# Second-stage 49x49 blocks on quarters of the TensorE array

## The chip, the cores and the metric

The kernel runs on one core of a Trainium2 chip. A core has five engines that work side by side, each through its own list of instructions in order: TensorE (PE: matmuls, 128 rows by 128 columns of multipliers), ScalarE (ACT), VectorE (DVE), GpSimd (POOL) and SyncE (SP, which here only issues DMAs). A matmul takes a stationary operand of up to 128 rows and 128 columns, streams up to 512 columns of a moving operand through it, and writes to PSUM, an accumulator memory of eight banks, each 128 partitions by 512 float32. ACT and DVE copy results from PSUM to SBUF. The metric is device time in microseconds.

## The reference

Two blocks follow each other, for eight batches of 3136 rows by 256 columns. The first is an attention whose weights are the squared positive part of the scores; the second projects its result three ways, convolves one projection with a long filter (by FFT over the 3136 rows), gates it twice and projects again.

```python
scores = (1.0 / S) * np.matmul(z, z.transpose(0, 2, 1))      # S = 3136, z has 64 columns
attn = np.maximum(scores, 0.0) ** 2
x = u * np.matmul(attn, v)
proj = x @ w_proj                                            # 256 -> 768
x1, x2, x3 = proj[..., :D], proj[..., D:2 * D], proj[..., 2 * D:]
x2_conv = np.fft.irfft(np.fft.rfft(x2, n=S, axis=1) * np.fft.rfft(filter_fft, n=S, axis=0)[None], n=S, axis=1)
out = (x1 * x2_conv * x3) @ w_out
```

## The kernel before

**Attention.** The columns of a batch's scores are cut into seven chunks (CHUNKS: five of 512, then 256 and 320), the rows into 25 tiles of 128. A *unit* of scores is two tiles (four in the chunk of 256) against one chunk. `score_mm` computes it with matmuls of 64 contraction rows: z is held twice, on partitions 0 to 63 and 64 to 127, so that one block uses the upper rows of the array and the next the lower rows, and each block goes to a bank of its own. A unit's two banks are one of three *pairs* (`ps_s`). ACT then takes the ReLU of both banks at once (tile R_t, line 1681), ACT or DVE squares it (A_t, lines 1688 and 1690), and `weigh` multiplies the squares with v into `ps_o`, two banks that collect a chunk. Scores are symmetric: some squares are turned by DMA transposes on SP's queue (M_t, M2e_t, M2o_t, line 1616) and used again in a later chunk. A short last tile of 64 rows goes through `weigh_short`.

**Projection and convolution.** A finished chunk becomes xT_t (line 1732), is projected with `wp` and gated (line 1062), and the part to convolve goes through a DFT in two stages, since 3136 is 64 x 49. Stage one (`dft1`, matrix T) is a full-array matmul; its result s_t goes to a scratch in DRAM (`spec`). When the seven chunks of a batch are through, `add_spectrum` reads the scratch back in another order (`load_spec`, tile spec_in_t). Stage two has 32 blocks of 49 x 49 per batch, each with 256 columns of real and imaginary parts side by side. `forward` multiplies the blocks of S, DVE multiplies with the filter's spectrum H (line 1161) and combines (1165, 1166), `inverse` multiplies the transposed blocks TZ, and the result gs_t goes to the scratch again (line 1212). In the last batch the combination is left out and `inverse2` does it by twice as many matmuls, with a negated copy of TZ (`make_minus`). `add_end` reads the second scratch, applies T4, gates (line 1255), multiplies with `wo` and stores.

**The second stage before.** Two blocks make one *slot* j of 16 (NJ). Their rows lie interleaved on 98 partitions (KR), and a stationary operand of 98 x 100 (KC) holds both blocks, with zeros where a row and a column belong to different blocks (`masks`). So a slot is one full-array matmul of 512 columns into one bank; slot 0, with the two frequencies that are their own mirror images, needs four matmuls of 256 columns and three more matrices (`sums`). `forward`, `inverse` and `inverse2` are called by tasks of kind FB that take one bank (`one_slots`); ACT or DVE copies it out (`both`).

**What sets the order.** No scheduler of the compiler is used. The class `Plan` holds estimated costs of all tasks and simulates the engines while it emits the instructions. `pick_pe` chooses what TensorE does next from queues of kinds: S (scores), W (weighted sums), FA, FB and FZ (projection, spectrum, ends). It starts a run of scores when two or three pairs of banks are free and stays in it while the next pair is. `go` adds 0.095 us where scores and other work follow each other. `Pairs` and `Singles` keep account of the banks of `ps_s`: a task takes a whole pair or one bank (MOST bounds the single ones). `pick` decides between ACT and DVE for jobs that both can do (YIELD weighs how long a job that only the other engine can do is held up).

**Lines of the profile.** All matmuls are issued by one helper and stand under line 468, transposes under 471; copies by ACT stand under 501 and by DVE under 505. In names, S and TZ are the matrices of stage two, zT_t the scores' operand, v_t the weighted sums' stationary operand.

Of the kernel before, what the change touches and what calls it, by code (L numbers as in the profile page):

```python
# [21 lines left out]
KR = 2 * N2  # L22
KC = 100
# [6 lines left out]
BACKLOG, AMPLE, STAY = 1.5, 5.0, 0.05  # L30
LATE_PUT, LATE_LOAD, LATE_TURN, LATE_C, LATE_D2 = 3.0, 1.0, 1.5, 2.5, 1.0
SPEC_LAG = 1
LATE_F = 6.0
AFTER = (1, 3, 5, 6)
FINAL = (0, 2, 4, 6, 1, 3, 5)
ZP, ZL = 0, 0.0
MOST = 3
FULL = INF
YIELD = 0.0
# [46 lines left out]
class Banks:  # L86
# [5 lines left out]
    def settle(self, k, t):  # L92
        self.at[k[0]][k[1]] = t

# [67 lines left out]
class Plan:  # L162


    def __init__(self):
        self.free = {e: 0.0 for e in ("PE", "ACT", "DVE", "SP", "POOL")}
        self.queues = {"S": [], "W": [], "FA": [], "FB": [], "FZ": []}
        self.pend = {e: [] for e in ("ACT", "DVE", "SP", "POOL")}
        self.credit = 0.0
        self.mode = None  # L170
        self.n = 0
        self.spare = []
        self.pairs = None
        self.bus = 0.0
# [74 lines left out]
    def pick_pe(self):  # L249
        t = self.free["PE"]  # L250
        got = {}
        for k, window in (("S", 1), ("W", 1), ("FA", 6), ("FB", 6), ("FZ", 6)):
            best = None
            for task in self.queues[k][:window]:
                s = max(t, self.ready_at(task))
                if s < INF and (best is None or s < best[0] - 1e-9):
                    best = (s, task)
            if best:
                got[k] = best
        if not got:  # L260
            return None
        more = self.queues["S"]
        if more and not more[0].left:
            left = self.backlog()
            if self.mode == "S":
                if "S" in got and got["S"][0] <= t + STAY:
                    return (*got["S"], "S")
                got.pop("S", None)
            else:
                want = 3 if left > AMPLE else 2  # L270
                free = self.pairs.when(min(want, len(more)) - 1)
                if "S" in got and free > t + 0.04:
                    rest = {k: v for k, v in got.items() if k != "S" and (k == "W" or left > BACKLOG)}
                    if rest and min(v[0] for v in rest.values()) < free:
                        got = rest
                    elif free < INF:
                        return max(got["S"][0], free), got["S"][1], "S"
            if not got:
                return None
        near = t + 0.04  # L280
        order = ["S"]
# [29 lines left out]
    def go(self):  # L311
        while True:
# [11 lines left out]
            if k:  # L324
                self.queues[k].remove(task)
                if (k == "S") != (self.mode == "S") and self.mode:
                    start += 0.095
                self.mode = k
# [10 lines left out]
def kernel(  # L339
# [133 lines left out]
    pair_slots, one_slots = Pairs(banks), Singles(banks)  # L473
# [132 lines left out]
    nc.gpsimd.iota(k1v, pattern=[[N2, N1 // 2], [0, 2]], base=0, channel_multiplier=0)  # L606
# [111 lines left out]
    pf, tp, odd, ge, php, n1p, pa, pb, r0, r1, m0, m1, half = (col[:, ds(i, 1)] for i in range(13))  # L718
    T1 = const.tile([P, P], BF16, name="T1")
    T4 = const.tile([P, P + N1], BF16, name="T4")  # L720
    NS = NJ + 3
    S2 = const.tile([P, NS, KC], BF16, name="S2")
    TZ = const.tile([P, NS, KC], BF16, name="TZ")
# [17 lines left out]
    def percol2():  # L741
        nc.vector.tensor_scalar(r1, pf, 0.5, -0.25, ALU.mult, ALU.add)
        nc.vector.tensor_scalar(r1, r1, RND, RND, ALU.add, ALU.subtract)
        nc.vector.tensor_scalar(tp, pf, 0.25, -0.375, ALU.mult, ALU.add)
        nc.vector.tensor_scalar(tp, tp, RND, RND, ALU.add, ALU.subtract)
        nc.vector.scalar_tensor_tensor(odd, tp, -2.0, r1, ALU.mult, ALU.add)
        nc.vector.scalar_tensor_tensor(r1, r1, -2.0, pf, ALU.mult, ALU.add)
        nc.vector.tensor_scalar(r0, r1, -1.0, 1.0, ALU.mult, ALU.add)
        nc.vector.tensor_scalar(tp, tp, -1.0, float(NT - 1), ALU.mult, ALU.add)
        nc.vector.tensor_tensor(m1, odd, r0, ALU.mult)  # L750
        nc.vector.tensor_tensor(m0, r0, m1, ALU.subtract)
        nc.vector.tensor_tensor(php, tp, r1, ALU.mult)
        nc.vector.tensor_scalar(php, php, float(NJ), float(QUART), ALU.mult, ALU.add)
        nc.vector.scalar_tensor_tensor(php, odd, -float(QUART), php, ALU.mult, ALU.add)
        nc.vector.tensor_single_scalar(half, pf, 0.0, ALU.is_equal)
        nc.vector.tensor_single_scalar(ge, pf, 25.0, ALU.is_equal)
        nc.vector.tensor_tensor(half, half, ge, ALU.add)
# [56 lines left out]
    s2_zero = on("POOL", lambda: nc.gpsimd.memset(S2[:].rearrange("p s m -> p (s m)").bitcast(F32), 0.0), 2.0, lat=0.3)  # L814
    after(s2_zero, 13.0)
    s2_done = []
    for j0 in (0, 8):
        box = {}

        def first(m, j0=j0):  # L820
            if j0:
                nc.vector.scalar_tensor_tensor(php, tp, 8.0, php, ALU.mult, ALU.add)
            nc.vector.tensor_scalar(m[:, 0 : 8 * N2], k2v, tp, php, ALU.mult, ALU.add)

        def masks(j0=j0, box=box):
            v = box["v"][:KR, 0 : 8 * N2].rearrange("p (j k) -> p j k", k=N2)
            a = int(j0 == 0)
            nc.vector.tensor_scalar(S2[:KR, ds(3 + j0 + a, 8 - a), 0:N2], v[:, a:], r0[:KR], None, ALU.mult)
            nc.vector.tensor_scalar(S2[:KR, ds(3 + j0, 8), 50 : 50 + N2], v, r1[:KR], None, ALU.mult)

        _, ta = sin_steps(box, 8 * N2, first, at=S2_AT)
        t = step("DVE", masks, 0.8)
        t.frees.append((ta, 0))
        if j0 == 0:
            join(t, s2_zero)
        s2_done.append(t)

    def q0_first(m):
        nc.vector.scalar_tensor_tensor(php, tp, -8.0, php, ALU.mult, ALU.add)
# [4 lines left out]
    def q0_masks():  # L844
        for i, msk, lo in ((3, m0, 0), (0, m0, 25), (1, m1, 0), (2, m1, 25)):
            nc.vector.tensor_scalar(S2[:KR, i, ds(lo, 25)], q0["v"][:KR, ds(lo, 25)], msk[:KR], None, ALU.mult)
        nc.vector.tensor_copy(S2[:KR, 2, 50:KC], S2[:KR, 3, 50:KC])

# [5 lines left out]
    for i0 in range(0, NS, 8):  # L854
        n = min(8, NS - i0)
        box = {}

        def turn(i0=i0, n=n, box=box):
            box["p"] = bank(BF16)
            for i in range(n):  # L860
                transpose(box["p"][:KC, ds(i * KR, KR)], S2[:KR, i0 + i, :], ident[:KR, :KR])

        def back(e, i0=i0, n=n, box=box):
            src = box["p"][:KC, 0 : n * KR].rearrange("p (s k) -> p s k", k=KR)
            copy(e, TZ[:KC, ds(i0, n), 0:KR], src)

        tt = pe("FB", turn, c_pe(*[P] * n), [s2_done[-1]], takes=[one_slots])
        tb = job(None, back, {"DVE": c_dve2(n * KR)}, [tt], prio=3)
# [3 lines left out]
    def halve():  # L872
        nc.vector.tensor_scalar(TZ[:KC, 0:4, 0:KR], TZ[:KC, 0:4, 0:KR], half[:KC], None, ALU.mult)

    tz_done.append(on("DVE", halve, 0.4, tz_done[:1], prio=3))
# [3 lines left out]
    def make_minus():  # L879
        minus.append(zT_p.tile())  # L880
        t = minus[0][:KC, 0 : NS * KC].rearrange("p (s k) -> p s k", k=KC)
        minus.append(t)
        nc.vector.tensor_single_scalar(t[:, :, 0:KR], TZ[:KC, :, 0:KR], -1.0, ALU.mult)

# [38 lines left out]
    def by_row(d):  # L923
        return d[0:S, :].rearrange("(p x) d -> p x d", x=2 * NJ)

    def load_spec(src, j0, nj, deps, late=0.0, home=l_p):
        box = {}

        def go():
            box["t"] = home.tile([P, 8, D] if home is l_p else [P, 4, D], BF16)  # L930
            nc.sync.dma_start(out=box["t"][:KR, 0 : 2 * nj, :], in_=by_row(src)[:, ds(2 * j0, 2 * nj), :])

        t = on("SP", go, 0.45, [*deps, *((d, ISSUED) for d in loads[-1:])], [home.slots], moves=0.6 * nj, late=late)
# [15 lines left out]
    def sums(ps, terms):  # L949
        for c, some in enumerate(terms):  # L950
            for k, (w, x) in enumerate(some):
                matmul(ps[:, ds(c * D, D)], w, x, start=(k == 0), stop=(k == len(some) - 1))

# [3 lines left out]
    def forward(ps, x, j):  # L957
        w = [S2[:KR, i, :] for i in range(NS)]
        if j:
            matmul(ps[:KC, :], w[3 + j], x, start=True, stop=True)  # L960
            return
        a, b = sides(x)
        sums(ps[:KC], (((w[3], a), (w[0], b)), ((w[1], a), (w[2], b))))

    def inverse(ps, y, j):
        w = [TZ[:KC, i, 0:KR] for i in range(NS)]
        if j:
            matmul(ps[:KR, :], w[3 + j], y, start=True, stop=True)
            return
        a, b = sides(y)  # L970
        sums(ps[:KR], (((w[3], a), (w[1], b)), ((w[0], a), (w[2], b))))

    def inverse2(ps, y, z, j):
        w = [TZ[:KC, i, 0:KR] for i in range(NS)]
        m = [minus[1][:, i, 0:KR] for i in range(NS)]
        (a, b), (c, d) = sides(y), sides(z)
        if j:
            sums(ps[:KR], (((w[3 + j], a), (m[3 + j], d)), ((w[3 + j], b), (w[3 + j], c))))
            return
        sums(  # L980
            ps[:KR],
            (
                ((w[3], a), (m[3], d), (w[1], b), (w[1], c)),
                ((w[0], a), (m[0], d), (w[2], b), (w[2], c)),
            ),
        )

    def c_line(j):
        return c_pe(2 * D) if j else c_pe(D, D, D, D)
# [12 lines left out]
    for j0 in range(0, NJ, 4):  # L1002
        ld, ibox = load_spec(DF, j0, 4, puts, LATE_F)
        for i in range(4):
            box = {}

            def mm(i=i, j0=j0, box=box, ibox=ibox):
                box["p"] = bank()
                x = ibox["t"][:KR, ds(2 * i, 2), :].rearrange("p c d -> p (c d)")
# [816 lines left out]
```

## Time and profile before

| | |
|---|---|
| median of 3 runs | 1012.26 us (1011.74 to 1012.39) |
| the profiled execution | 1012.86 us |
| its span, first to last instruction | 1011.0 us |
| granted clock of TensorE over the span | 0.997 of full speed |
| matmuls recorded | 5,958 (weight loads: 6,046) |
| matmuls of scores, 64 rows, 512 columns | 776 |
| second stage, 512 columns, forward (spec_in_t, S) | 122 |
| second stage, 512 columns, inverse (xh, TZ) | 105 |
| ReLU of 1024 columns on ACT | 408 x 1.031 us |
| squares of 1024 columns: on ACT, on DVE | 195 x 1.070 us, 197 x 1.221 us |
| HBM read and written | 142 GB/s over the span |

A group of the profile reads: line, engine, operation, output tile and input tiles, shape, count, busy time, mean of one. A matmul's shape stands as rows*columns of the stationary operand, then partitions x columns of the moving one. Some records of matmuls are missing (compare the count of weight loads), and a matmul's recorded duration includes a modelled end, so that matmuls that follow each other overlap in the table: what one costs is the distance from start to start. In the timeline, a row merges instructions of one group that follow each other: start, length, engine, group, count.

### The profile page before, as it was taken

What the parts mean: (1) busy time and instruction counts of PE and PEld (TensorE: products, weight loads), DVE (VectorE), ACT (ScalarE), POOL (GpSimd) and SP (SyncE); (2) the same over time, 40 slices, a digit from 0 to 9 for tenths busy, and PEclk for the clock granted to TensorE, in tenths of its full rate; (3) what the DMA queues carried; (4) which work ended last, traced back from release to release, by engine and by line L of the source; (5) the groups of instructions that cost most, each with busy time, mean ns of one, the idle gap of its engine ahead of it and who ended that gap; (6) DMA issues with size and microseconds to landing.
All of it is one profiled execution on the core that took longest, in us unless ns stands there. A gap on an engine that the chain in (4) does not pass through costs nothing.

```text
span 1011.0 us, 17656 instructions
## 1 busy us (share of the span) xinstructions
PE 967.4 (96%) x5958; PEld 490.8 (49%) x6046; DVE 787.6 (78%) x1424; ACT 907.9 (90%) x1231; POOL 188.7 (19%) x401
## 2 busy tenths in 40 slices
PE   6999999998999999999999999999999999999985
PEld 2344544455444564445544464445644455444654
DVE  7976779866797777887788777897769877797675
ACT  6988899998999899998999989998899989999774
POOL 5142311131011310123112131112201222000000
PEclk9999999999999999999999999999999999999998
DMA  9799868878978887987989889897888779977656
GB/s 167 141 175 171 160 132 163 161 155 172 181 165 168 167 182 163 175 136 150 213 180 161 154 180 211 144 187 168 194 166 169 153 133 207 201 142 162 132 187 207
DMA packets 331770, 170.18 MB, mean 168 GB/s; under 512 B 241160, under 2 KB 306504, under 8 KB 331680
## 3 DMA queue, kind: packets, MB, share of 16 engines
q1 hardware_dynamic: 303952, 138.09, 62.3%
q0 software_dynamic: 27728, 30.97, 21.1%
q8 instruction: 47, 0.77, 0.3%
q14 instruction: 43, 0.35, 0.1%
HBM read 90.26 MB, written 53.35 MB: 142 GB/s over the span
## 4 chain that ended last, share of the span: by engine, by line
PE 76%; DVE 8%; ACT 8%; issue 3%; DMA 3%; SPq 1%; ACTq 0%; DVEq 0%
PE ps_o_t L468 42%; PE ps_s L468 33%; ACT R_t L1681 5%; DVE A_t L1690 3%; ACT A_t L1688 2%; DVE xh L1161 1%; DVE xT_t L1732 1%; DMA out_dram<-ost_t 1%; DMA ost_t<-in_z_dram 1%; DMA M_t<-A_t 1%; DMA A_t<-spec 1%; SPq L593 1%; DVE yT_t L1255 0%; DVE R_t L1161 0%; ACT s_t L501 0%
## 5 line engine op out<-in xcount | busy, mean ns | idle before, releaser
L1681 ACT ACTIVATE R_t<-ps_s 128x1024 f32<-128x1024 f32 (+4 forms) x512 | 471.0, 958 | 43.9 <-PE ps_s L468 40.3
L468 PE MATMUL ps_o_t<-A_t,v_t 128*128 128x512 bf16 (+3 forms) x1998 | 461.7, 353 | 8.9 <-DVE A_t L1690 4.0
L468 PEld LDWEIGHTS <-v_t 128*128 128x128 bf16 x2826 | 254.3, 98 | 254.3 <-issue 59.4
L1690 DVE TENSOR_TENSOR A_t<-R_t 128x1024 bf16<-128x1024 f32 (+3 forms) x250 | 280.0, 1130 | 123.3 <-ACT R_t L1681 122.0
L1688 ACT ACTIVATE A_t<-R_t 128x1024 bf16<-128x1024 f32 (+3 forms) x246 | 243.2, 995 | 4.6 <-DMA M_t<-A_t 1.3
L468 PE MATMUL ps_s<-zT_t 64*128 64x512 bf16 (+2 forms) x1064 | 148.7, 356 | 4.8 <-ACT ost_t L501 2.7
L551 POOL COPY tick<-xT_t 1x1 bf16<-1x1 bf16 x54 | 14.0, 259 | 727.1 <-DVE xT_t L1732 727.1
L468 PE MATMUL ps_s<-xT_t,wp 128*128 128x512 bf16 (+2 forms) x418 | 102.3, 352 | 3.9 <-DVE xT_t L1732 1.9
L1732 DVE SCALAR_TENSOR_TENSOR xT_t<-ps_o_t,uT_t 128x256 bf16<-128x256 f32 (+2 forms) x224 | 76.1, 382 | 19.3 <-PE ps_o_t L468 18.5
L501 ACT ACTIVATE x_t<-ps_s 128x512 bf16<-128x512 f32 (+2 forms) x143 | 77.2, 572 | 15.4 <-PE ps_s L468 9.3
L468 PEld LDWEIGHTS <-zT_t 64*128 64x128 bf16 (+1 forms) x1081 | 43.4, 94 | 96.0 <-issue 81.0
L1161 DVE TENSOR_TENSOR xh<-xh,H 100x1024 bf16<-100x1024 bf16 x120 | 80.9, 683 | 3.7 <-ACT xh L501 3.3
L1062 DVE TENSOR_TENSOR gate_t<-ps_s,x_t 128x256 bf16<-128x256 f32 (+2 forms) x214 | 70.2, 382 | 16.9 <-PE ps_s L468 12.1
L468 PE MATMUL ps_o_t<-M_t,v_t 128*128 128x512 bf16 (+2 forms) x352 | 82.0, 353 | 0.1
L468 PEld LDWEIGHTS <-wp 128*128 128x128 bf16 x448 | 42.2, 97 | 48.5 <-issue 11.9
L1255 DVE TENSOR_TENSOR yT_t<-ps_s,gate_t 128x512 bf16<-128x512 f32 (+2 forms) x99 | 59.3, 619 | 3.5 <-PE ps_s L468 2.8
L542 POOL DMA_DIRECT2D un_t<-in_u_dram x112 | 60.0, 556 | 8.3 <-issue 6.1
L561 POOL DMA_DIRECT2D v_t<-in_v_dram x112 | 59.5, 553 | 4.1 <-issue 1.8
L468 PE MATMUL ps_s<-wp,xT_t 128*128 128x256 bf16 x398 | 56.4, 273 | 0.1
L468 PE MATMUL ps_s<-wo,yT_t 128*128 128x256 bf16 (+1 forms) x358 | 53.5, 273 | 1.4 <-DVE yT_t L1255 0.9
L501 ACT ACTIVATE xh<-ps_s 100x512 bf16<-100x512 f32 (+1 forms) x85 | 50.3, 632 | 2.3 <-PE ps_s L468 2.2
L505 DVE CAST x_t<-ps_s 128x512 bf16<-128x512 f32 (+2 forms) x70 | 44.6, 648 | 9.0 <-PE ps_s L468 7.1
(154 smaller groups left out, 884.6 us busy)
## 6 DMA issues: line engine op xcount, KB each, us to landing
out_dram<-ost_t SPq DMA_DIRECT2D x66, 256.0 KB
spec<-s_t SPq DMA_DIRECT2D x96, 128.0 KB
spec_in_t<-spec SPq DMA_DIRECT2D x28, 392.0 KB
spec<-gs_t SPq DMA_DIRECT2D x28, 392.0 KB
v_t<-in_v_dram POOLq DMA_DIRECT2D x80, 128.0 KB, 4.3
un_t<-in_u_dram POOLq DMA_DIRECT2D x80, 128.0 KB, 4.6
conv_in_t<-spec SPq DMA_DIRECT2D x33, 256.0 KB
out_dram<-ost_t SPq DMA_DIRECT2D x19, 128.0 KB
```

Of the source, the lines that this page charges most:

```text
L468: wrote(nc.tensor.matmul(o, *args, **kw), o)
L501: got = nc.scalar.activation(out_, in_, AF.Copy)
L505: got = nc.vector.tensor_copy(out_, in_)
L542: nc.gpsimd.dma_start(out=t[ds(j * N1, N1), lo - t0 : hi - t0, :], in_=x[:, n2 : n2 + hi - lo, :])
L561: nc.gpsimd.dma_start(out=t[ds(j * N1, N1), ds(v_at(a), (b - a) * D)], in_=r[:, n2 + a - lo : n2 + b - lo, :].rearrange("p t d -> p (t d)"),)
L1062: got = nc.vector.tensor_tensor(g[:, ::-1] if h == 0 else g, p, x, ALU.mult)
L1161: nc.vector.tensor_tensor(x[:, 1 - i], x[:, 0], h, ALU.mult)
L1255: got = nc.vector.tensor_tensor(yb["y"][:, dh, 0:w], p, gates[b, c, dh][:, 0:w], ALU.mult)
L1681: has_read(nc.scalar.activation(blocks(box["R"], n, cw)[:rows], p, AF.Relu), p)
L1688: nc.scalar.activation(a, r, AF.Square)
L1690: nc.vector.tensor_tensor(a, r, r, ALU.mult)
L1732: nc.vector.scalar_tensor_tensor(x, f, inv_s2, ut, ALU.mult, ALU.mult)
```

## The change

The second stage is laid out anew. The 49 rows of one block lie on partitions 0 to 48, those of the next on 64 to 112. A *unit* of four blocks is two slots: the block in row half h and slot c uses the 64 x 64 part of the array at rows h*64 and columns c*64, streams 512 columns and writes to partitions c*64 and up of bank h of a pair. The masks are gone, S2 holds the blocks as such, and three small matrices S0 and T0Z serve the two special frequencies. Where a unit has more than one matmul per part, the four parts take turns.

```diff
+    def quads(ps, plan_of):
+        todo = [(h, c, plan_of(h, c)) for h in range(2) for c in range(2)]
+        for n in range(max(len(x) for _, _, x in todo)):
+            for h, c, x in todo:
+                if n < len(x):
+                    cols, w, m, start, stop = x[n]
+                    matmul(ps[ds(c * N1, N1), h, cols], w, m, start=start, stop=stop)
...
-    def forward(ps, x, j):
-        w = [S2[:KR, i, :] for i in range(NS)]
-        if j:
-            matmul(ps[:KC, :], w[3 + j], x, start=True, stop=True)
-            return
-        a, b = sides(x)
-        sums(ps[:KC], (((w[3], a), (w[0], b)), ((w[1], a), (w[2], b))))
+    def forward(ps, x, i):
+        def of(h, c):
+            at = ds(h * N1, N2)
+            w, m = S2[at, 2 * i + c, :], x(c)[at]
+            if i or h or c:
+                return whole(w, m)
+            a, b = sides(m)
+            v = [S0[at, k, :] for k in range(3)]
+            return sums((((w, a), (v[0], b)), ((v[1], a), (v[2], b))))
+
+        quads(ps, of)
```

`inverse` and `inverse2` change likewise. A unit is a task of a new kind Q, which takes a pair of banks and is copied out by two jobs, one for each bank (`Half` and `Halves` free each bank by itself). The same function serves the filter, the forward and the inverse pass:

```diff
+    def add_quads(mm, ev, cost, deps, takes):
+        box = {}
+
+        def go():
+            box["p"] = ps_t[plan.got[0][1]]
+            mm(box["p"])
+
+        a = pe("Q", go, cost, deps, [pair_slots, *takes])
+        evs = []
+        for h in range(2):
+            e_ = job(None, lambda e, h=h: ev(e, h, box["p"][:, h, :]), both(2 * D), [a])
+            e_.frees.append((Half(a, half_slots, h), 0))
+            evs.append(e_)
+        return a, evs
```

Units are put into runs of scores. When a run begins and a unit is due (`soon`), the whole run goes on quarters: each score matmul of 128 stationary columns is issued as two of 64 columns, and so is the short last tile.

```diff
+            o = blocks(ps, len(pair), cw)[:, i]
+            for m in range(0, P, N1 if plan.quarters else P):
+                n = N1 if plan.quarters else P
+                matmul(o[ds(m, n)], zt[h, ds(t * P + m, n)], zt[h, ds(C0[at], cw)], start=True, stop=True)
```

In `pick_pe`, while a run on quarters lasts, one unit follows the first score unit (LEAD = 1, `quad_run`), and more only when no scores are left; other work comes after. `go` now counts 0.12 us for leaving a run on quarters.

```diff
+        quad = got.pop("Q", None)
+        if self.mode == "S" and self.quarters and quad and quad[0] <= t + STAY:
+            if not more or self.quad_run < 1 and self.score_run >= LEAD:
+                return (*quad, "Q")
...
-                if (k == "S") != (self.mode == "S") and self.mode:
-                    start += 0.095
-                self.mode = k
+                half = k in ("S", "Q")
+                if half != (self.mode == "S") and self.mode:
+                    start += 0.095 if half or not self.quarters else 0.12
+                    self.quarters, self.quad_run, self.score_run = half and self.soon, 0, 0
```

Loads and stores of the second stage become two DMAs of 49 rows each on SP's queue instead of one of 98:

```diff
-            nc.sync.dma_start(out=box["t"][:KR, 0 : 2 * nj, :], in_=by_row(src)[:, ds(2 * j0, 2 * nj), :])
+            for r in range(2):
+                nc.sync.dma_start(
+                    out=box["t"][ds(r * N1, N2), 0 : 2 * nj, :], in_=by_row(src, r)[:, ds(2 * j0, 2 * nj), :]
+                )
```

The planner's constants change too, and with them the order of all engines and the share of ACT and DVE: a run of other work may go on while a smaller backlog of weighted sums is left, a third free pair is no longer asked for, projection work ranks first only while ACT's and DVE's queues are short (FULL), a job goes to the second engine only if it holds up less there (YIELD), and a store of a result counts as landing later (LATE_OUT).

```diff
-BACKLOG, AMPLE, STAY = 1.5, 5.0, 0.05
+BACKLOG, AMPLE, STAY = 1.0, 99.0, 0.05
...
+LATE_OUT = 2.0
...
-MOST = 3
-FULL = INF
-YIELD = 0.0
+MOST = 4
+FULL = 3.5
+QUAD, FIRST, LEAD = -INF, 0.0, 1
+YIELD = 1.0
```

The rest of the diff builds the matrices: the first stage's columns are numbered so that a row half holds one kind of block, the phases of the blocks are computed without masks, and `halve`, `make_minus` and the transposes that make TZ follow the new shapes. The filter products run on 128 partitions instead of 100.

## The prediction

> **What bounds the kernel now.** I began with the busy shares and the chain of waits on the page of the kernel before.
>
> ```profile
> PE 967.4 (96%) x5958; PEld 490.8 (49%) x6046; DVE 787.6 (78%) x1424; ACT 907.9 (90%) x1231; POOL 188.7 (19%) x401
> ...
> PE 76%; DVE 8%; ACT 8%; issue 3%; DMA 3%; SPq 1%; ACTq 0%; DVEq 0%
> ```
>
> TensorE (PE) is busy 96% of the span and carries 76% of the chain. A matmul's recorded end is modelled (about 0.38 us for 512 columns), so its real price must be read from start to start, in the timeline of TensorE:
>
> ```profile
> 518.41 0.60 PE L468 MATMUL ps_s<-wo,yT_t 128*128 128x256 bf16 x4
> 518.85 0.60 PE L468 MATMUL ps_s<-spec_in_t,S 98*100 98x256 bf16 x4
> 519.38 0.41 PE L468 MATMUL ps_s<-wo,yT_t 128*64 128x256 bf16 x2
> 519.72 1.04 PE L468 MATMUL ps_o_t<-A_t,v_t 128*128 128x512 bf16 x4
> 520.69 0.82 PE L468 MATMUL ps_s<-zT_t 64*128 64x512 bf16 x6
> 521.44 1.04 PE L468 MATMUL ps_o_t<-A_t,v_t 128*128 128x512 bf16 x4
> ...
> 525.24 0.38 PE L468 MATMUL ps_s<-spec_in_t,S 98*100 98x512 bf16 x1
> 525.46 1.89 PE L468 MATMUL ps_o_t<-A_t,v_t 128*128 128x512 bf16 x8
> 527.28 0.82 PE L468 MATMUL ps_s<-zT_t 64*128 64x512 bf16 x6
> ```
>
> Four things stand here. (1) A second-stage matmul (98x100, names S and TZ) goes among full-array matmuls at the same price as they do: 525.24 to 525.46 is 0.22 us, though half of its stationary block is zeros; four of 256 columns take 0.44 (518.41 to 518.85). Single starts give 0.2155 us for 512 columns and 0.109 for 256. (2) Score matmuls, 64 rows each, run two at a time: six take three steps. (3) Each change between the full array and row halves costs extra: 525.46 to 527.28 is 1.82, eight steps are 1.724, so 0.096 are left; the way back (520.69 to 521.44) is 0.75 against 0.647. Over all single starts the medians are 0.096 in and 0.093 out, 0.189 for one run of scores. (4) The two 128x64 matmuls, the only ones that use half of the columns, take 0.34 us to the next full one (519.38 to 519.72): two steps of 0.109, a change of 0.096, and 0.026 that is left.
>
> Now the budget. The order of TensorE's instructions has 2,588 full steps of 512 columns, 1,373 of 256, 428 paired steps of 512 and smaller ones: 906.2 us at the prices above (0.136 for 320 columns, 0.056 for 128). It has 213 runs on row halves (40.3 us) and 8 on column halves (1.7). That is 948.2 of the span's 1011.0; 62.8 us are start, tail, waits and rounding. So TensorE is the bound nearly everywhere, and what is taken off it counts, except where another engine rules. Two stretches show where that is:
>
> ```profile
> 500.00:960.00 460.00, 453.40 (x2801) 230.93 (x2841) 366.48 (x642) 426.29 (x576) 76.60 (x163) 1.00 0.84 170
> 960.00:1011.00 51.00, 36.57 (x288) 25.45 (x287) 31.92 (x66) 30.98 (x61) 0.00 (x0) 0.95 0.63 195
> ```
>
> The columns after the length are PE, PEld, DVE, ACT and POOL. TensorE is full to 960 and not after it. The chain in that tail reads:
>
> ```profile
> 970.61 1.09 ACT xh L501 x2
> ...
> 977.39 0.68 DVE xh L1161
> 978.07 0.60 DVE R_t L1161
> 978.67 0.60 DVE xh L1161
> ...
> 989.40 0.43 SPq L943
> 989.88 5.90 DMA A_t<-spec
> ```
>
> Here VectorE's filter products rule, and then a round trip through DRAM.
>
> **The change, part by part.** *Blocks removed and added.* One pass over a batch's spectrum is 15 matmuls of 512 and four of 256 columns: 15 x 0.2155 + 4 x 0.109 = 3.67 us. There are 18 such passes (filter 1, forward 8, inverse 7, and the last batch's inverse, which counts twice): 66.1 us. The order agrees: 240 full steps of 512 and 132 of 256 columns vanish. A pass is now seven units of one step of four matmuls and a first unit of four steps of 256: 7 x 0.2155 + 0.436 = 1.945, and 35.0 us for 18, if the four parts run side by side. Difference **-31.1 us**. Two parts on different rows do run side by side (point 2). Two parts on the same rows with different columns do not occur before; the bounds are 0 and, where they go one after the other, another 0.2155 us per step. I take 0, from the row pairs, the nearest row; the other end is a rival.
>
> *Changes of mode.* The units aren't free riders. In the order of the changed kernel there are 144 runs on row halves and 121 on quarters, 265 instead of 213: 52 x 0.189 = **+9.8 us**. A score run goes on quarters from its first block when a unit is due, so no third kind of change occurs within a run. Quarters load 64 columns. By point 4 such a run shows 0.026 us once, ahead of its first matmul, and nothing at the second: 121 x 0.026 = **+3.1**. Bounds: 0, if another part hides it, and 4 x 0.026 per run (12.6 us) if the four loads go in single file; further 0.026 for each of the 385 quarter steps (10.0), if loads are never hidden. I take the observed single one.
>
> The Trainium skill, "TensorEngine Tiling (Array Packing)", section "Restrictions and Gotchas", says that column tiling switches the fast weight load off. The 0.026 us in point 4 is what this trace shows of it; with the rule applied to each step the sum would be worse by the 10.0 us just named.
>
> *Scores.* They cost the same steps as before with twice the instructions, where they run on quarters. Starts of a pair lie 3 ns apart now, so eight instructions (four loads) in 0.2155 us are hidden; uncovered, 0.003 x 385 x 2 = 2.3 us.
>
> *Evictions.* Two copies of 512 columns per unit, as many as before: 0.61 us on ACT, 0.687 on DVE, and 100 or 98 partitions cost as much as 128 (0.632, 0.684). What moves is the squares: in the order, 79 of 1024 columns go from ACT (1.070) to DVE (1.221), and some 47 copies of 512 go back. ACT becomes about 840 us, DVE about 861: both below TensorE's 930, so no cost, but a square on DVE comes 0.151 later (a rival).
>
> *DMAs.* A load or store of a spectrum is two DMAs of 49 rows, some 76 more on SP's queue, at 0.45 us each 34 us. That queue issues about 565 of 1011 us, mostly mirror transposes. TensorE waits for loads from that scratch twice today, 1.4 us in all, and what lies behind on the queue is mostly a transpose that is used a chunk later; I take 0 up to the tail. There the last store and load stand on the chain: **+0.5**. Uncovered throughout, 34. Setting up the blocks loses five short DVE instructions, hidden behind other work of the first 100 us: 0.
>
> *Tail.* Three of the 18 passes belong to the last batch, 3 x 1.73 = 5.2 us, and run where DVE rules: that gain I don't count, **+5.2**.
>
> Sum: -31.1 + 9.8 + 3.1 + 0.5 + 5.2 = -12.5 us. The profiled span would be 998.5, its run 1012.86 - 12.5; against the median of 1012.26 this is **999.7 us**. Ends: with no exposed loads and the tail counted, -21.3 (about 991); with all loads exposed, +7 (about 1019).
>
> **The rivals.**
> - *More gain.* ACT, at 90% now, gets 7% lighter, and its waits on TensorE's banks shrink with the tail gain: 985 to 989. Against it: TensorE's longest waits today are 3 to 5 us. Chance 0.06.
> - *Waits eat it.* The 79 squares on DVE are each 0.151 us later and a weighted sum behind waits: 79 x 0.151 = 11.9, and the time is about 1011.6. For it: DVE goes from 78 to 86%. Against: TensorE waits for DVE's squares 4.0 us in all today, eight times. Chance 0.08.
> - *Exposed loads*, as above, near 1019. Against: full-array loads (98 ns each) vanish under matmuls 0.2155 apart. Chance 0.06.
> - *Pairs of banks (slower).* A second-stage block took one bank of six and now needs both banks of one of three pairs, which scores need too; both are freed by two copies. If each of 136 units held the next scores up for half a copy (0.3 us), that is 41 us: 1040. It decides from 12.5/136 = 0.09 us per unit. For it: the 512 ReLUs already hold pairs for about 1 us each. Against: TensorE waits for banks only a few us in all. Chance 0.07.
> - *Columns in single file (slower).* The two column parts of one row half go one after the other, the scores on quarters too: 385 x 0.2155 = 83 us, 1083. It decides from 0.033 us per step. No row before has two column parts at once. Chance 0.04.
>
> The Trainium skill, "TensorE: Matmul & The Clock Gate", section "Part 3: Packing small matmuls — row/col tiling", says that a weight load overlaps matmuls only if its row group differs, which speaks for this last rival. The trace does not bear that out for the full array, where loads of all rows are hidden under running matmuls.
>
> That the change doesn't do what it says is excluded by the order: every unit has four quarter matmuls.
>
> **How the numbers follow.** The forecast (989 to 1009) has 0.69. Below 989: 0.06. The range 988 to 1013 adds the waits' case and part of the exposed loads, and leaves out some 0.04 below and 0.15 above. About 0.2% (2 us) is what a measurement can tell from no change: faster 0.77 (forecast, more gain, part of the waits), same 0.06 (the rest of the waits), slower 0.17 (loads, pairs, single file). The likeliest case's own range is 989 to 1009.
>
> **What would show it.** Right: quarter matmuls in fours that start within some 10 ns, 0.22 us from one four to the next, 0.19 to 0.22 us lost per run, PE still the chain's main part up to 960, ACT and DVE near 840 and 861 us. Wrong: fours 0.43 us apart (single file); more than 0.1 us lost at the entry (loads); PE idle ahead of scores behind copies (pairs) or ahead of weighted sums behind DVE's A_t (waits); or a tail that got shorter by 5 us.

## The result, and the profile after

The changed kernel takes 1015.65 us (median of 22 runs, 1010.01 to 1025.29); the kernel before, run beside it, 1011.16 us (22 runs, 1007.85 to 1019.68). The ratio is 1.0041, with a 95% interval of 1.0021 to 1.0060: slower by some 4 us, where 12.5 us less were forecast. The profiled execution took 1014.12 us, its span is 1012.0 us, and the mean granted clock is 0.988.

The page of the changed kernel, busy shares and chain:

```profile
PE 969.6 (96%) x6776; PEld 472.2 (47%) x6776; DVE 851.8 (84%) x1470; ACT 854.2 (84%) x1182; POOL 187.5 (19%) x403
...
PE 72%; DVE 11%; DMA 7%; ACT 5%; issue 3%; SPq 1%; ACTq 0%; DVEq 0%
```

ACT and DVE are loaded nearly as foreseen (840 and 861 us forecast). TensorE's share of the chain fell from 76% to 72%, and DMA's rose from 3% to 7%: the chain leaves TensorE more often, and it goes to transfers. The timeline of TensorE shows the quarters (start, length, engine, line, group, count):

```profile
517.69 0.41 PE L518 MATMUL ps_s<-zT_t 64*64 64x512 bf16 x4
517.93 0.39 PE L518 MATMUL ps_o_t<-As_t,v_t 64*64 64x512 bf16 x4
518.14 0.39 PE L518 MATMUL ps_s<-spec_in_t,S 49*64 49x512 bf16 x4
518.36 0.39 PE L518 MATMUL ps_s<-zT_t 64*64 64x512 bf16 x4
518.68 1.90 PE L518 MATMUL ps_o_t<-A_t,v_t 128*128 128x512 bf16 x8
```

Four 64 x 64 matmuls take what one full one took: from 517.93 to 518.14 and to 518.36 are 0.21 and 0.22 us. The whole run, 517.69 to 518.68, is 0.99 us for four steps of 0.2155, so 0.13 us are lost within it and on the way out. So the mechanism works, and the time must have gone elsewhere. DVE makes xT_t once per tile, the same 224 times in both kernels and in the same order, so the 29th, 92nd, 148th and 218th of them serve as landmarks that both traces have. They part each span into the start, three stretches and the tail. The windows, first of the kernel before (columns: window, length, busy time and count of PE, PEld, DVE, ACT, POOL, granted clock, DMA share, GB/s), without the first 143.3 us, which are the start:

```profile
143.30:410.10 266.80, 259.25 (x1570) 128.43 (x1592) 208.84 (x372) 246.17 (x328) 47.83 (x103) 1.00 0.82 166
410.10:648.40 238.30, 235.25 (x1459) 120.31 (x1481) 190.56 (x340) 222.61 (x300) 47.76 (x98) 1.00 0.89 173
648.40:950.50 302.10, 297.53 (x1829) 149.79 (x1857) 243.95 (x424) 280.78 (x379) 50.97 (x109) 1.00 0.82 167
950.50:1011.00 60.50, 46.07 (x364) 32.11 (x362) 36.53 (x77) 37.35 (x71) 0.00 (x0) 0.96 0.65 188
```

and of the changed kernel, whose start takes 145.5 us (the first two rows are the windows that the prediction showed of the kernel before):

```profile
500.00:960.00 460.00, 451.84 (x3191) 220.48 (x3189) 392.43 (x664) 402.63 (x554) 74.72 (x163) 1.00 0.89 168
960.00:1012.00 52.00, 36.58 (x347) 23.48 (x345) 32.10 (x63) 28.50 (x56) 0.00 (x0) 0.80 0.61 192
145.50:406.40 260.90, 257.89 (x1823) 123.45 (x1820) 228.54 (x391) 231.51 (x321) 49.83 (x103) 1.00 0.91 174
406.40:649.00 242.60, 237.79 (x1661) 115.00 (x1658) 208.18 (x356) 211.38 (x289) 45.47 (x98) 0.99 0.92 171
649.00:945.20 296.20, 292.13 (x2072) 141.89 (x2072) 256.74 (x427) 264.11 (x364) 49.75 (x109) 1.00 0.88 168
945.20:1012.00 66.80, 51.21 (x465) 33.69 (x462) 41.02 (x85) 38.10 (x72) 0.00 (x0) 0.84 0.58 179
```

The first and the third stretch became 5.9 us shorter each, as a gain spread over the kernel would make them. The second became 4.3 us longer, and the tail (950.5 to the end before, 945.2 to the end after) 6.3; the start took 2.2 more: 2.2 - 5.9 + 4.3 - 5.9 + 6.3 = +1.0, the difference of the spans. So it is a loss in two places, the second stretch and the tail, and not a dearer matmul. Inside the second stretch the timeline of all engines has one place that stands out:

```profile
554.73 6.54 SPq L1692 DMA_TRANSPOSE M_t<-A_t  x1
...
561.69 0.43 DVE L1460 COPY zd_t<-zn_t 128x1024 bf16<-128x1024 bf16 x1 [3.30 <-DMA zT_t<-zd_t]
...
562.49 1.06 ACT L1766 ACTIVATE A_t<-R_t 128x1024 bf16<-128x1024 f32 x1 [0.30 <-DMA M_t<-A_t]
562.63 0.75 DVE L1810 SCALAR_TENSOR_TENSOR xT_t<-ps_o_t,uT_t 128x256 bf16<-128x256 f32 x2
...
563.44 0.61 PE L518 MATMUL ps_o_t<-M2e_t,v_t 128*128 128x512 bf16 x2 [2.24 <-DVE xT_t L1810]
```

Read it from the top. One mirror transpose keeps SP's queue 6.54 us from issue to the next instruction, where the mean over all 260 transposes is 1.6 us. DVE's copy into zd_t waits 3.30 us for a transpose of the same queue; the products xT_t that free the collecting banks stand behind that copy on DVE; and TensorE's next weighted sum waits 2.24 us for them. A late transfer of SP's queue has reached TensorE in two steps, through an engine that was not the bound. The transpose that the copy waits for was issued at 546.21 us, ahead of the 6.54 us one, so it did not stand behind it. It stands right behind two stores of gs_t, issued at 545.43 and 545.83, and landed late itself: 15.4 us after its issue, by the completion events that the trace keeps of each DMA. The transfers as a whole were slow then, as the windows show, first of this kernel, then of the run with single stores in experiment 5 (the DMA share is the packets' time over that of 16 engines, and can exceed 1):

```profile
550.00:555.00 5.00, 5.00 (x45) 2.25 (x43) 4.97 (x9) 4.76 (x7) 0.00 (x0) 1.00 1.28 91
555.00:560.00 5.00, 5.00 (x36) 1.89 (x35) 3.35 (x6) 5.00 (x8) 0.00 (x0) 1.00 1.30 88
...
550.00:555.00 5.00, 4.84 (x45) 2.30 (x43) 4.97 (x9) 4.76 (x8) 0.00 (x0) 1.00 1.11 217
555.00:560.00 5.00, 5.00 (x36) 1.96 (x29) 4.95 (x11) 5.00 (x8) 0.00 (x0) 1.00 1.19 225
```

The DMA engines are at least as busy and move less than half as much; in these 10 us of the changed kernel single packets of 256 bytes took up to 4.2 us.

In the tail the chain is (start, length, what):

```profile
982.95 0.40 SPq L1285
...
983.39 0.51 SPq L1285
...
984.33 0.55 SPq L1285
...
984.99 0.95 SPq L1285
...
985.99 3.93 DMA spec<-A_t
...
990.00 2.67 DMA A_t<-spec
```

The last stores of gs_t stand on SP's queue one behind the other, each twice, and the load of the next stage can't begin before the last has landed. From the end of DVE's last product with H to the issue of that load it takes 4.6 us in the kernel before (984.28 to 988.91) and 8.8 here (981.15 to 990.00).

### The profile page after: what moved, and what is told of

It reads as the page before. It is cut to its first block, busy times and chain, and to the rows that moved or that the text cites. A ratio compares the mean times of both kernels' runs of the same rounds, so it can differ in the third digit from the quotient of the medians.

```text
span 1012.0 us, 19360 instructions
## 1 busy us (share of the span) xinstructions
PE 969.6 (96%) x6776; PEld 472.2 (47%) x6776; DVE 851.8 (84%) x1470; ACT 854.2 (84%) x1182; POOL 187.5 (19%) x403
## 4 chain that ended last, share of the span: by engine, by line
PE 72%; DVE 11%; DMA 7%; ACT 5%; issue 3%; SPq 1%; ACTq 0%; DVEq 0%
PE ps_o_t L518 41%; PE ps_s L518 31%; DVE A_t L1768 5%; ACT R_t L1759 3%; DVE xT_t L1810 2%; DMA zT_t<-zd_t 2%; DMA M2e_t<-A_t 1%; ACT A_t L1766 1%; DVE xh L1240 1%; DMA spec_in_t<-spec 1%; DMA M_t<-A_t 1%; DMA conv_in_t<-spec 1%; DMA ost_t<-in_z_dram 1%; ACT gs_t L551 1%; DMA un_t<-spec 0%
## 5 line engine op out<-in xcount | busy, mean ns | idle before, releaser
L1759 ACT ACTIVATE R_t<-ps_s 128x1024 f32<-128x1024 f32 (+4 forms) x512 | 476.8, 960 | 79.9 <-PE ps_s L518 37.6
L1768 DVE TENSOR_TENSOR A_t<-R_t 128x1024 bf16<-128x1024 f32 (+3 forms) x337 | 379.9, 1145 | 56.0 <-ACT R_t L1759 45.7
L518 PEld LDWEIGHTS <-v_t 128*128 128x128 bf16 (+2 forms) x2872 | 247.6, 98 | 280.4 <-issue 87.4
L518 PE MATMUL ps_s<-zT_t 64*64 64x512 bf16 (+4 forms) x1436 | 174.5, 370 | 1.4 <-ACT R_t L1759 0.6
L1766 ACT ACTIVATE A_t<-R_t 128x1024 bf16<-128x1024 f32 (+4 forms) x159 | 153.0, 965 | 6.7 <-DMA M_t<-A_t 3.0
L551 ACT ACTIVATE x_t<-ps_s 128x512 bf16<-128x512 f32 (+2 forms) x169 | 91.8, 582 | 24.5 <-PE ps_s L518 19.1
L518 PEld LDWEIGHTS <-zT_t 64*64 64x64 bf16 (+1 forms) x1469 | 54.7, 100 | 119.6 <-issue 105.5
L1240 DVE TENSOR_TENSOR xh<-xh,H 128x1024 bf16<-128x1024 bf16 x120 | 81.7, 682 | 2.3 <-ACT xh L551 1.5
L518 PE MATMUL ps_o_t<-M2e_t,v_t 128*128 128x512 bf16 (+1 forms) x192 | 46.9, 356 | 6.3 <-DVE xT_t L1810 6.2
L551 ACT ACTIVATE s_t<-ps_s 128x512 bf16<-128x512 f32 (+1 forms) x74 | 43.6, 599 | 6.4 <-issue 2.1
```

The costliest lines, as they stand in the source:

```text
L518: wrote(nc.tensor.matmul(o, *args, **kw), o)
L551: got = nc.scalar.activation(out_, in_, AF.Copy)
L1240: nc.vector.tensor_tensor(x[:, 1 - i], x[:, 0], h, ALU.mult)
L1759: has_read(nc.scalar.activation(blocks(box["R"], n, cw)[:rows], p, AF.Relu), p)
L1766: nc.scalar.activation(a, r, AF.Square)
L1768: nc.vector.tensor_tensor(a, r, r, ALU.mult)
```

## The experiments

Three suspects were left: the twofold DMAs on SP's queue, the clock in the tail, and the planner's constants. All ratios are to the kernel before, run on the same chip beside them.

**1. The kernel before with twofold DMAs, and nothing else.**

```diff
-            nc.sync.dma_start(out=box["t"][:KR, 0 : 2 * nj, :], in_=by_row(src)[:, ds(2 * j0, 2 * nj), :])
+            for r in range(2):
+                nc.sync.dma_start(out=box["t"][ds(r * N2, N2), 0 : 2 * nj, :], in_=by_row(src)[ds(r * N2, N2), ds(2 * j0, 2 * nj), :])
```

(and the store likewise)

> The kernel before, with each second-stage load and store issued as two DMAs of 49 rows instead of one of 98; the order of all engines is as before. Theory 'queue' (76 more DMAs on SP's queue make its transposes late, and the changed kernel's 2 us waits of TensorE at 87 and 563 us come from that): SP's issue time rises from 565 us towards 645, issues over 2 us from 26 towards 47, time 1.004 to 1.010 of before. Theory 'clock' (the loss is in the tail, where the granted clock falls to half) and theory 'planner' (the new constants send 79 squares to DVE): within 0.2% of before, issue time up by 76 x 0.45 = 34 us at most.

Measured: 1.0049 (1.0026 to 1.0072). The DMAs alone cost about 5 us, in the same bytes and packets. In its profile the start, the three stretches and the tail stand +3.1, -0.9, 0.0, -0.4 and +6.5 us against those of the kernel before: here the start and the tail pay, the middle doesn't. (This profile, at 1021.1 us, is the slowest of the run's 12 executions; their median is 1017.37.)

**2. The clock in the tail.** In the tail of the changed kernel the clock is granted at half from 970.8 to 984.4 us, which the windows show:

```profile
955.00:970.00 15.00, 12.37 (x118) 8.09 (x117) 10.65 (x25) 10.23 (x20) 0.00 (x0) 1.00 0.37 108
970.00:985.00 15.00, 13.69 (x146) 7.61 (x143) 12.14 (x21) 11.75 (x23) 0.00 (x0) 0.54 0.68 226
```

Before, it is full until 1005.8. Quarter steps are over sooner, so TensorE streams less there. Two full-array matmuls of 512 columns ahead of each of the last batch's 16 units, into the unit's own bank, were to keep it up; another run has one.

```diff
+    def warm(ps, final):
+        for _ in range(2 * final):
+            matmul(ps[:, 0, :], T1[:, :], H[:, 0].rearrange("p c d -> p (c d)"), start=True, stop=True)
```

> The changed kernel with two full-array matmuls of 512 columns into a unit's own bank ahead of each of the last batch's 16 units (their results are overwritten). Theory 'clock': TensorE stays busy enough in the tail, the granted clock stays at 1.0 from 960 to 985 us, and the time falls by 4 to 7 us against the changed kernel (ratio to before 0.997 to 1.000). Theories 'queue' and 'planner': the tail waits for loads and VectorE, the fillers (16 x 0.62 = 10 us of TensorE) hide at best, ratio 1.004 to 1.010.

> The changed kernel with one full-array matmul ahead of each of the last batch's 16 units instead of two. Theory 'clock': it costs half of the fillers' time and the clock stays at 1.0 from 960 to 985 us: ratio 0.999 to 1.002. If the clock falls all the same or the tail is bound by VectorE and loads: 1.003 to 1.006.

Measured: 1.0031 (1.0001 to 1.0062) with two, 1.0063 (1.0038 to 1.0087) with one. Neither interval lies apart from that of the changed kernel (1.0021 to 1.0060).

**3. The planner's constants**, each way: the kernel before with the new ones, and the changed kernel with the old ones.

```diff
-BACKLOG, AMPLE, STAY = 1.5, 5.0, 0.05
+BACKLOG, AMPLE, STAY = 1.0, 99.0, 0.05
...
-FULL = INF
-YIELD = 0.0
+FULL = 3.5
+YIELD = 1.0
```

(MOST and LATE_OUT too; the second run has it the other way round)

> The kernel before with the changed kernel's planner constants (BACKLOG, AMPLE, MOST, FULL, YIELD, LATE_OUT) and nothing else. Theory 'planner': squares move to DVE here too, and the time rises to 1.01 or more. Theories 'queue' and 'clock': within 0.3% of before, or a little faster, since ACT at 90% is relieved.

> The changed kernel with the planner constants of before. Theory 'planner': faster than the changed kernel, 0.985 to 0.995 of before. Theories 'queue' and 'clock': 1.000 to 1.010, as the changed kernel or slower.

Measured: 1.0082 (1.0051 to 1.0113) and 1.0156 (1.0118 to 1.0195). The new constants harm the kernel before by 0.8% and help the changed one by over 1%: they are fitted to it, so they are no reason for its loss.

**4. One DMA instead of two in the changed kernel.** The scratch's rows are read and written as 98 neighbouring partitions, 0 to 97, so one DMA does. The values then stand on other partitions than the quarters expect: this run doesn't compute the reference's result, and its lower row half contracts 34 rows instead of 49 (streamed columns, and so steps, are the same).

```diff
-            for r in range(2):
-                nc.sync.dma_start(
-                    out=box["t"][ds(r * N1, N2), 0 : 2 * nj, :], in_=by_row(src, r)[:, ds(2 * j0, 2 * nj), :]
-                )
+            nc.sync.dma_start(out=box["t"][: 2 * N2, 0 : 2 * nj, :], in_=by_row(src)[:, ds(2 * j0, 2 * nj), :])
```

(and the store likewise); a second run has the two fillers of experiment 2 as well, a third is the changed kernel once more, for a second profile of it.

> The changed kernel with each second-stage load and store as one DMA of 98 rows again, the bytes and the order of the engines unchanged; the rows land on partitions 0 to 97 instead of 0 to 48 and 64 to 112, so the second stage's values aren't the reference's, and the lower row half contracts 34 rows, at the same price. Theory 'queue' (two DMAs for one cost 0.49% in the kernel before): SP's issue time falls from 645 to about 580 us, the 256-byte packets of the transposes from 27.6 to about 25 ns, the waits of 2 us at 87 and 563 us go, and the ratio to before is 0.994 to 0.999. Theory 'clock' alone: the ratio stays at 1.003 or more.

> The same with two full-array matmuls ahead of each unit of the last batch. Theories 'queue' and 'clock' together: 1 to 2 us below after_onedma, since the fillers' work was as long as the waits that they took away. If only the queue counts: as after_onedma or up to 5 us slower.

> The changed kernel once more, for a second profile. Theory 'queue': TensorE waits over 1 us for the same places again (near 87, 563 and 592 us), where the mirrors and the xT products come late; theory 'clock': half clock again for over 10 us between 960 and 985 us. A profile without either says that the first one was an accident.

Measured: 0.9948 (0.9930 to 0.9967), and 0.9953 (0.9938 to 0.9969) with fillers. Undoing the twofold DMAs turns the slower kernel into a faster one. The fillers do what they should, here in the windows of that run,

```profile
955.00:970.00 15.00, 13.60 (x137) 6.46 (x134) 10.94 (x21) 10.04 (x20) 0.00 (x0) 1.00 0.66 218
970.00:985.00 15.00, 13.00 (x133) 5.78 (x132) 11.22 (x24) 10.15 (x20) 0.00 (x0) 1.00 0.52 155
```

and gain nothing: the clock, which the run without them has at half from 965.9 to 979.5 us, stays full, and the time is the same. So lifting the clock by fillers doesn't pay; what the half clock costs by itself isn't shown, since it can't be parted from what the fillers cost. The second profile of the changed kernel took 1018.5 us (span 1016.4) and has its second stretch at 247.7 us, again long, again through waits between 535 and 600 us; in the run with one DMA that stretch is 237.0. It is no accident: over all profiles with the changed order, the second stretch is 242.6, 247.7, 246.4 and 245.4 us in the four that send both stores through SP's queue (the two profiles of the changed kernel and the two of experiment 2), and 237.0 to 238.4 in the five others (experiments 4 and 5). In each of the four TensorE waits for late xT_t between 561 and 568 us (1.3 to 2.7 us), and for R_t of ACT between 591 and 597 (1.2 to 3.6); in the five others the longest wait of TensorE from 525 to 605 us is 1.1.

**5. Loads or stores, transfer or queue?** Three runs part what is left. One makes only the stores single (they write other values than the reference's; loads and products are as in the changed kernel). Two keep everything and send the second DMA, of each load and store or of each store alone, through GpSimd's queue.

```diff
# stores single
-                    for r in range(2):
-                        nc.sync.dma_start(
-                            out=by_row(D2[b % 2], r)[:, ds(2 * j0, 2 * per), :], in_=gx["g"][ds(r * N1, N2), 0 : 2 * per, :]
-                        )
+                    view = D2[b % 2][0:S, :].rearrange("(p x) d -> p x d", x=2 * NJ)
+                    nc.sync.dma_start(
+                        out=view[:, ds(2 * j0, 2 * per), :], in_=gx["g"][: 2 * N2, 0 : 2 * per, :]
+                    )
# second store on GpSimd's queue
-                        nc.sync.dma_start(
+                        (nc.gpsimd if r else nc.sync).dma_start(
```

> The changed kernel with each second-stage store as one DMA of 98 rows (partitions 0 to 97, so the stored values aren't the reference's), the loads still two. If loads and stores cost alike: the ratio lies midway between 1.004 and 0.995, near 0.9995. If the stores are what delays (the tail's last stores stand in series): 0.996 to 0.998. If the loads: 1.001 to 1.004.

> The changed kernel with the second DMA of each second-stage load and store issued by GpSimd's queue instead of SP's; nothing is left out and the order is unchanged. Theory 'SP' (what costs is that 76 more DMAs stand in SP's one queue, ahead of mirror transposes and in the tail's last stores): SP's issue time falls to about 575 us, the waits at 563 us go, and the ratio to before is 0.994 to 0.999. Theory 'transfers' (smaller DMAs are slower wherever they are issued, and slow the transposes' packets): packets of 256 bytes stay near 27 ns and the ratio at 1.002 to 1.006.

> The changed kernel with the second DMA of each second-stage store on GpSimd's queue and both loads on SP's; nothing is left out. Theory 'SP': as after_onestore within 0.2%. Theory 'transfers': 1.002 to 1.006, above after_onestore.

Measured: stores single 0.9947 (0.9929 to 0.9965); both seconds on GpSimd's queue 0.9980 (0.9964 to 0.9996); second stores alone there 0.9967 (0.9951 to 0.9984). Single stores give all that single DMAs give, more than any of the expectations allowed, so the twofold loads cost nothing that can be measured. The windows of the run with single stores, whose start takes 144.5 us:

```profile
144.50:405.10 260.60, 255.25 (x1796) 123.59 (x1820) 228.76 (x391) 231.56 (x321) 49.84 (x103) 1.00 0.89 173
405.10:643.10 238.00, 233.51 (x1637) 114.85 (x1658) 208.41 (x356) 211.12 (x290) 45.48 (x98) 1.00 0.89 176
643.10:938.60 295.50, 289.31 (x2041) 141.84 (x2071) 256.68 (x426) 264.15 (x364) 49.75 (x109) 1.00 0.85 168
938.60:1003.10 64.50, 49.13 (x463) 32.33 (x463) 40.86 (x85) 37.95 (x72) 0.00 (x0) 0.89 0.61 185
```

Against the changed kernel the second stretch is 4.6 us shorter and the tail 2.3; the others move by 0.3 to 1.0. (Some matmul records of this run are missing, as the counts of matmuls and loads show.) The page of the run with second stores on GpSimd's queue shows the move:

```profile
L1285 POOL DMA_DIRECT2D spec<-gs_t x30 | 16.1, 535 | 233.5 <-ACT gs_t L551 170.0
...
spec<-gs_t POOLq DMA_DIRECT2D x28, 196.0 KB, 4.0
spec<-gs_t SPq DMA_DIRECT2D x28, 196.0 KB
```

The same rows are moved by as many DMAs; where they queue differs, and into how many packets they are cut (2,624 in place of 2,016). Its second stretch is 238.1 us, as short as without them, while its tail stays long (67.5): there the two halves of the last stores are waited for either way. It computes everything and is faster than both kernels: 1009.59 us beside 1012.39 us.

What the stores do to SP's queue, summed from the traces of five kernels:

| | before | before, twofold | after | stores single | second stores on GpSimd |
|---|---|---|---|---|---|
| DMAs issued by SP | 633 | 709 | 709 | 673 | 673 |
| time of issue, us | 564.7 | 612.1 | 644.5 | 595.3 | 614.2 |
| of it 260 transposes, us | 363.8 | 385.8 | 410.1 | 379.7 | 388.7 |
| issues of over 2 us | 26 | 35 | 47 | 31 | 41 |
| longest issue from 530 to 570 us, us | 3.0 | 3.7 | 6.5 | 2.8 | 3.3 |
| mean 256-byte packet, ns | 24.5 | 27.3 | 27.6 | 26.3 | 27.2 |
| such packets of over 1 us | 323 | 591 | 740 | 633 | 610 |
| mean of all the others, ns | 22.5 | 22.4 | 21.3 | 20.8 | 21.7 |
| second stretch, us | 238.3 | 238.3 | 242.6 | 238.0 | 238.1 |
| tail, us | 60.5 | 67.0 | 66.8 | 64.5 | 67.5 |

From "stores single" to "after" 36 DMAs are added, and the time of issue grows by 49.2 us, 1.37 us for each. The stores' own part of that is small: two of 49 rows take 0.39 us each to issue, one of 98 takes 0.48, so 36 x 0.31 = 11.1 us. 30.4 us fall on the transposes, whose number and bytes stay (theirs are the 256-byte packets), the rest on other DMAs. The packets' pace as such does not change: their median is 18 ns in all five traces. What raises the mean are some hundred packets, of 220,032, that take over 1 us. The last column, which moves the same rows, keeps 41 long issues, but not the very long ones about 550 us, and its second stretch is short. The transpose that held DVE up (zT_t<-zd_t, the one near 545 us) landed 15.4 us after its issue in the changed kernel and 14.4 in its second profile, but after 8.1 us with single stores, 8.8 with the second stores on GpSimd's queue and 5.7 with single DMAs. So these traces put the loss of that stretch to a few very late transposes, held up by a few very slow packets; why those packets were slow isn't shown.

## Why the prediction was wrong, point by point

The sum can be held against the trace item by item. TensorE's steps, counted from the matmuls of the traces at the prediction's prices, went from 906.2 to 874.6 us and the changes of shape from 41.5 to 54.3: together -18.8, where the prediction had -31.1 + 9.8 + 3.1 = -18.2. What is left of the span, waits above all, grew from 63.3 to 83.1 us: +19.8, where the prediction had +5.7 (0.5 for DMAs, 5.2 for the tail). The matmul half was right, the wait half was not.

- *Blocks on quarters, -31.1.* Right. The matmuls of a four start about 3 ns apart, and fours follow each other at 0.24 us (the first two of a run) and 0.218 (medians). The rival of columns in single file is refuted. The Trainium skill ("TensorE: Matmul & The Clock Gate", section "Part 3: Packing small matmuls — row/col tiling") says that a weight load overlaps running matmuls only if its row group differs. This trace does not agree: four matmuls on zT_t, on both row halves, begin at 553.086 us, and the loads of TZ for the next four, on the same rows, at 553.113, 0.21 us ahead of their matmuls.
- *Changes of mode, +9.8.* Right: medians 0.309 us from the last full matmul to the first quarter and 0.308 back, start to start, so 0.093 each beyond the step.
- *Loads of a quarter run, +3.1 (0.026 each).* Right: a quarter run loses 0.127 to 0.131 us over its steps, one on row halves 0.106, so 0.022 to 0.025 more. The rival of exposed loads is refuted.
- *Pairs of banks.* Refuted: TensorE waits for banks behind ACT's R_t 1.8 us in all, against the 41 us of that rival, as the waits of TensorE show (who waits <- for whom: us in all, times, longest; the first two lines are of the kernel before, the next three of the changed one, the last of the run with single stores). In the second profile it is 5.8 us, most of it about 583 and 596 us.

```profile
PE ps_o_t L468 <- DVE A_t L1690: 4.0, 8, 0.9
...
PE ps_o_t L468 <- DVE xT_t L1732: 0.6, 2, 0.4
...
PE ps_o_t L518 <- DVE xT_t L1810: 8.4, 10, 2.3
...
PE ps_o_t L518 <- DVE A_t L1768: 4.5, 10, 0.6
...
PE ps_s L518 <- ACT R_t L1759: 1.8, 4, 1.2
...
PE ps_o_t L518 <- DVE xT_t L1810: 5.7, 9, 1.8
```

- *Squares on DVE.* Refuted as a cause: TensorE waits 4.5 us for A_t, against 4.0 before; and the changed kernel with the old constants, where DVE makes 192 squares of 1024 columns instead of 276, is the slowest of all.
- *DMAs: "I take 0 up to the tail ... +0.5".* This is the step that failed. The price of 0.45 us for each was on the safe side (0.39 for a store); that it is hidden was not true. The argument was that what lies behind on the queue is mostly a transpose used a chunk later. But the queue's slack was shared by all transposes, and the extra stores cost the transposes nearly three times what they cost themselves (30.4 against 11.1 us of issue); now and then a transpose is late enough to stop DVE, and then TensorE. TensorE's waits for xT_t show a part of it: 8.4 us in all, where it was 0.6 before, but 5.7 of them stay with single stores and belong to the changed order. Undoing the stores is worth 1.0041 - 0.9947 = 0.94%, about 9.5 us (0.0094 x 1011) of the 16.6 between forecast and measurement (-12.5 against +4.1, which is 0.41% of 1011.16). The bound of 34 us was named, and its hidden end taken.
- *Tail, 5.2 not counted.* The gain indeed did not come, but the tail became longer, by 4.0 us with single stores and by 6.3 with twofold ones. By events, with the run of single stores between the other two: from the last landmark to the first load of stage two 15.3, 17.1 and 17.0 us (before, single, after); from there to the first load of the last stage 23.1, 23.5 and 27.8; from there to the end 22.1, 23.9 and 22.0. The twofold stores fall into the middle one. The other 1.8 us twice were not traced to a cause.

With single stores the three stretches together changed by -6.2 - 0.3 - 6.6 = -13.1 us, against the -13.0 that the prediction makes without its DMA term. So the theory of TensorE held where TensorE rules, and start and tail gave back 5.2 of it in that span. That the two agree to 0.1 us is luck. The -13.0 also holds a part of the start, and TensorE's own terms, counted for each stretch at the prediction's prices, are -3.7, -2.6 and -5.2 us, -11.5 in all: the first and the third stretch gave more than that, the second, even with single stores, 2.3 less.

What stays open: why the middle is hit between 535 and 600 us and not elsewhere (the kernel before with twofold DMAs pays at the ends alone); the start, 0.8 to 3.4 us longer in all variants with the changed order, the one with single DMAs too, where a weighted sum waits 1.7 to 2.3 us near 87 us; and the 1.8 us of the tail. About 7 us of the 16.6 lie there, and no run was made that parts them. The stretches are read from single traces, and the spans of the changed kernel's two profiles differ by 4.4 us.

One rival to the number of DMAs was not tested. Every twofold DMA is also one of 49 rows. The traces record 8 completion events for each of those, 15 for one of 98 rows and 16 for every other DMA on SP's queue; and a store of 49 rows lands a median of 4.5 us after its issue, one of 98, with twice the bytes, 3.5 us. So a DMA of 49 rows may be spread less widely, and this, not the second place in the queue, may be what makes packets late. Two DMAs of 98 rows and half the columns each would part the two; no run has them.

## What to carry to other kernels

A queue that is 56% occupied isn't free: before adding DMAs to it, look at the longest instruction on it and at who waits for what stands behind, since the cost appears at others' instructions, not in the added ones' own time. A layout that is served by two DMAs where one did before has a price that belongs to the layout; try the second one on another engine's queue first (here it gave back 0.7% of the time). When a sum says "hidden", give the two ends of that term as much weight in the range as the terms that are sure.

## What the runs showed of the hardware that was not expected

Matmuls on different parts may start out of program order: in the trace of the changed kernel a quarter matmul on zT_t begins at 137.800 us, ahead of one of 256 columns (spec_in_t, S) that stands earlier in the order and begins at 137.907. The granted clock fell to half after some 3.4 us that TensorE's steps, a quarter matmul counted as a quarter of one, fill to 0.32 (970.8 us, though matmul records are busy for 0.69 of them) or 0.26 (994.7 us). One fall in the run with one filler came at 0.44, and the kernel before kept its clock through such a stretch at 0.45 (to 995.6 us): too close for these runs to give a threshold. And the packets of DMA transposes become slower with more stores beside them by their tail alone: the median stays at 18 ns, while packets of over 1 us went from 323 to 740 of the same 220,032.
